# A hand-planned order for a delta-rule layer and a SwiGLU layer: the groups of tiny products ahead of K's turn removed, and the order searched anew

## The chip, the cores and the metric

The kernel runs on one core of a Trainium2 chip. The metric is the time of one execution on the device in microseconds (us); the runs of the kernel before have a median of 670.19 us over three executions (669.39 to 670.93). The core has five engines with a queue each: TensorE (PE, matrix products), VectorE (DVE), ScalarE (ACT), GpSimd (POOL) and SyncE (SP, which here issues most of the transfers). Every engine works through its own queue strictly in the order in which the program wrote it, and waits at the head of that queue for whatever the next instruction needs.

## The reference

```python
def _attn_ref(q, k, v, beta):                 # 4 batches, 8 heads, 768 steps, 48 channels
    k_n = k / (np.linalg.norm(k, axis=-1, keepdims=True) + 1e-06)
    state = np.zeros((B, H, D, D)); y = np.zeros_like(q)
    for t in range(S):
        kt, vt, bt = k_n[:, :, t], v[:, :, t], beta[:, :, t, None]
        y[:, :, t] = einsum('bhd,bhde->bhe', q[:, :, t], state)
        v_old = einsum('bhde,bhd->bhe', state, kt)
        state = state + bt[..., None] * einsum('bhd,bhe->bhde', kt, vt - v_old)

def _moe_ref(x, w_gate, w_val, w_out, rms_g): # x: y as 3072 tokens x 384; 384 -> 1536 -> 384
    xn = x / sqrt(mean(x * x) + 1e-06) * rms_g
    g = xn @ w_gate
    return (g * sigmoid(g) * (xn @ w_val)) @ w_out
```

All data are float32 in the result; the three weight matrices come as float64 and are converted on the chip.

## The kernel before, in words

The 768 steps are cut into 12 chunks of 64 (`NCH`), and each chunk is solved for all 32 heads at once. For a chunk the program normalises k (`norms`), turns k and q so that their channels lie on the partitions (`turn`, a product with the identity, whose line is L560), forms the scores of k against k and of q against k, inverts a triangular 64 by 64 matrix per head, and from that computes the chunk's y and the new state (`recur`). The two first chunks invert with `invert`, the later ones by a longer way in `prep`. Then the SwiGLU layer runs on the chunk's 256 tokens: `ffn_plain` (products L1443 and L1425) in chunks 0 and 1, and in chunks 2 to 11 `ffn` (products L1538) and `down` (products L1595), which need fewer products for more additions on VectorE; the sums that feed L1595 are L1587. The weights are loaded in 18 pieces into seven raw buffers and converted to float32 by two operations on ScalarE (L500, L501), a shift on VectorE (L495) and an addition on POOL (L498) each (`weights`).

Nothing of this is issued where it is written. Every step is an operation of a class `Plan`: an engine, a planned duration, a function that issues it, and the keys that it reads and writes. At the end `Plan.run` takes all operations in the order that a string `ORDER` spells out, two characters for the number of an operation in the order of creation (base 90). There is one string for all engines; each engine's queue is what remains of it for that engine. Before it issues them, `Plan.times` works out planned start times from the planned durations, from a model of the transfers' landings and from a model of how TensorE's instructions are fetched. These times have one effect on the program: which PSUM bank an operation gets, and where *filler* is put. Where the plan leaves PE idle for over 0.8 us in the first 110 us (`UNTIL`), it issues useless wide products with the identity into a free bank (L1714; 4, 2 or 1 times 128 columns), so that they fill the planned gap. Ahead of PE's first operation, where the time since the previous one is counted from 0.0, `fillers` returns a fixed list.

The function `ahead` adds an operation of twelve useless products of one column (L642); `prep` calls it six times in chunk 0. Each counts as 48 of the units in which the plan counts PE's instructions. The order string puts five of the six groups at the very start of PE's queue, ahead of the two halves of K's turn of chunk 0 (L560 on k), and the sixth between the two halves of q's turn.

Around these, the first chunk goes: the transfers of k (one half issued by SP, one by ACT); ScalarE squares k (L604) and VectorE sums the squares (L605); K's turn, copied out of PSUM by ScalarE (L572) and VectorE (L570); scores (L700); a power on POOL for the norm (L609); the transposition and the inversion on VectorE (L734 to L814; L810 is `back`, the transposition back); two rounds of products (L841, L874) and additions (L881); V times beta over the norm (L1155); the products L1212, L1236 and L1190; the mean square and the scale of y (L1308, L1348); y's turn (L1371) and its scaling (L1380); and then the first product of the SwiGLU layer (L1443).

Of the kernel before, what the change touches and what calls it, by code (L numbers as in the profile page):

```python
# [16 lines left out]
C = 64  # L17
W = 32
# [18 lines left out]
    "&-&I%m%,&L'+&(&N%/%'%+%l%j&S%1%k%B&M%-(+&,'$%p'%'G%>&O%q'V''%(%o%r&X%0%n%G'H%2&P#8(*%s#7$~%?#6%@%C'J%u%#&T%w'K%9%t&U"
    "'&&Q%5&R%A%x%4'I&Y%L%z&V%v%y(1%E%D&^#:%:%F&.#;&Z'(%{&['L%|%}%;','M&W%<'N&_'-'P'Q(,%6&`'O&]%M%7'R'/%N&d#9(-#5&a#<'.&6"
    "(.&c)#'0%H%O(/)$&h'S)%&/%J&e&b)&&i%P&f%I&j'T(0&g'1)d&k'A'2&0%K'3&n'C'4'B'W*G&l&7)e'U)g'5'D&o'X'6&s&p'Y'E'Z)f&1'8'[&t"
    "'F)h']'7&q'='^'9&m'_':'>&u'?'`'@)i';'<'a)A&:)k&v)j&8&r'b)l'c)n(?)o'd)m(;(2'e&;(@'f&9'g&w'h(<'i'j&x)''k)q)0)p(=&y(A'l"  # L40
    "(>)C(B(C)1'o(3'm(D'p)2'n(I)B(E)3(7(J)r(F(4(K)(&}&z(N&~(6'w(L'|)=(O'y)s'z)t'}(5(G(S'~(P'{)u(H'x*F)v)w(T't)x'u)y's(#'q"
    "(Q(U)z(M'r($'v){*M(%)|*N(R(()}()'#(&(9(')D)~&|)G(V)E*#(W)I)H)F*$*H(X*%(:(^&2*&(Y*I*J*')J(Z*(*K*)(_**([*+)b,v(c)K(`(8"
    "*,(a(d*L*-)L(h,/)c*/)M*.(e(i*0(f)4,u,2)>(j,0)N(m,1)O)5,3*5))+i*7(k*<*O,4*9*;)?(]*=,5*>,6*:)*(n,A,:)+,B,9),(r,7)6(o,8"
    ")P+k)Q*8(s(p*1)-*3)7*?*2).)V*6)8)R*4)W(b)X,;)9*@(t,<)/)S)T*A*U)Y):)U(g)Z*C);*D*B)[*E+j(l)](u)^+l)<)_)`+o)a+m,=*P,>*V"
    ",?*W,@,w,C*R*S,D(q*Q&{,E,F&3,G,x,H(v,I+p,y,J(w,K*T,z,L*Y,M*[*Z,N*X(x*],O+q*^(|,{*d(}(y(~*_._*`({*e(z*f*a.`*l,P*b.a+&"
    "*g*m,Q*j*n,R*k.b+(,S*o,}*h*p,T,|*v*q+**c,U.c*z++*w*r*i*{+)+2,V*|+n*~*}*x,W+'.d+.,X*s+,,Y,~*t+r,Z+-+3+4+#,]+/+$.e+:*y"
    ",[+%+8+5,^+;*u,_+<+s+9+t/L+@+=+v+>.f+6+u+D+A+w.g+?,c+B)@,j-#,k.i,m+y+H+E,l.h,h+0+L.t+I.j.l,-+x+M,i+F+z.m+7+~+G+{.k+T"
    "+N+C,#,./K,$+J+1.u,b+O+P,g,n,%+|,`+Q+}.;,a+K,o-$.o,p,e,&.=,d+V+R,q,f,',t,(.n+U,),s+S&4,r,*+Z,+.<,,+].>-%+W+^.A.?-*.p"
    ".B.q-,.r/M.s.v+X.C.w+[.x.@.y.z/N.{&5+a.|-(+Y/O.}-&.~/P.D/#+b/$-+--+_/%.^1~+d/Q-..E15+`-0.F-/.].G+e-116/&-)17/'-2+f.H"
    "+c-T+h-3.I+g-6/(18.K-8-7-4.J-</).L->/S/*-=-V-9-?19/+-B-:2#-@-5-C.M-X/,-L-;-Y/--A-D1:-M-W-'-H/.-N/R-O-]-I-U.N-a//-J-E"  # L50
    "/0-P1;-b-Z/1-Q-i-R-[-^/3-c-K/5-S-g1<.O0n/2-h-d/4-j-m-_-e-F1=-n/C-G-k/B/T1?.P1>-o-f-l-`1B-w-p1C-s1@-x1A.'.#-y/X-q-t/A"
    "-z/@-u-r1J.$/>-{/?-v.(/D1E-|/U1D.Q-}/8.)/9-~.R.%/6.S.&/E/<./.T/=1K.U/:.-.V.W/;.X.Y.Z.[.+...0/7/Z0p1F/W1G/F1H/V.31I1L"
    "0o/I/H1M.*/G1N/J1O1P.,1Q0t.41R.11S1T2$1U0v/]1V0q.2/^2%.72&1W0r0u2'1X/_.81Y.9/a/`.51Z0w2)/b0s.61[.:/c2*2(0x/[3h/i0y/d"
    "0z/e/j0{3i/k1]0|4T/q1^0~0+/f/l0-/g0}1_3k/m/o1`1#/s3j/p1a/Y/r0/1b/t/h/u1c3l00/{/v1d/w1$/|0#/n/}1e130.1g070$0'2+3m0%1%"
    "030&1f140,2,081h0(012-0)3D/x3n021q/y0?/~21/z041&090@0*1v0=1u0:4U0E3E0;1j3o0>0A1l051'0<0C060B1i1s3p0D1t0F1r0I3r3q0M0J"
    "3}3u1w0N3t0Q0U3s0O0G3v0Y0P1x0R0K1k1o0L0S0H1m1(1y1n1p0[0V1)3w1z0T1{0W3x1}0b1*1+0`1|0X0Z1,3~1-1.1/100^110a3F0c123J3y3G"
    "3K3z3{0]0f3|4V4#4$0_4%3H4&4'4(0d4W4)0g4X4*0h4+4[234Y4,2/25244-0i27260e4.29284/2;4Z0j2:206>2<2.2?0k406?2A0m2@0l2E2B2^"
    "412F2C2G423I6A2K6@2H43222`2L2I442M452J6B3L2U2D4]2N2b2V2Q462W2a2X3M2=472_6C482O2>492R2d3N2S2Y4:3O2c3Q2e2j3P2Z6D2l2T3R"
    "4>2[2k2f4<2m3T2r3S2g2n3U2t2P2s3g4=6E2p4;2u2h2]2|4^2q4L6F2i3V2o2v3f4K6H6G2x2w6K4_2y6I2}6J3$2z6L2{4E3(3%3W307+3&3)2~6S"
    "3#3'6N3*4a5w313,3X3+326M3.3-4@4I384H365y4J333/3Y344G37394A6T4C5x6O4F6P4M4D6Q3<4B6R3Z6U4N4?356V7,6W4`3[6X6Y3]4b3^6Z4O"  # L60
    "3=723:6[4S3_4d4Q6]4R3`4P3a3b5}3;3c6^5z6_3@7-3d3e5~6#6`5{4e4f7.3A3C4h7/6a4g3B5|4j736b4i703?544k6c3>4l6d4n6e4r716$4m8q"
    "4s4o4t6%8r6&4z8s6f6'4c4x6(4u4{566g6)4y4|6h8t4~6i9_4}4p586j6+6*5#5(4v6,6k5,4w6l5)8u5$4q576<6m59506=5-8M5%5.6q5/5@6-51"
    "558v5&5A525:6o5*746n5<6p5;755=535B8w5+6.5F9^5C5H5'7#5G775J8N6s5I6~5>5L8x5K6z9*6/5N6v5M9+5R6y6{8y6|5S6}5O5V5T608z768{"
# [193 lines left out]
def kernel(  # L257
# [37 lines left out]
    ident = sbt("ident", [128, 128])  # L295
# [171 lines left out]
    def weights(first, last):  # L467
# [14 lines left out]
        for n, (dst, src, keys) in list(enumerate(todo))[first:last]:  # L482
# [19 lines left out]
            P.add("DVE", 0.7, shifted, pr, w=cak)  # L502
# [134 lines left out]

    def ahead(n, pr):

        def small():  # L640
            for _ in range(n):
                nc.tensor.matmul(banks[0][0:32, 0:1], ident[:, 0:32], ident[:, 0:1])  # L642

        P.add("PE", 0.04 * n, small, pr, r=["ident"], size=4 * n)
# [39 lines left out]
    def invert(c, pr):  # L684
# [127 lines left out]
        P.add("DVE", 1.02, back, later(8), r=["two16"], w=["acc16", "xc16"], port=False)  # L812
# [72 lines left out]
    def prep(c):  # L885
# [826 lines left out]
    def filler(n, warm):  # L1712
        for w_ in n:
            nc.tensor.matmul(  # L1714
                warm[:, 0 : 128 * w_].rearrange("p (w n) -> p w n", n=128), ident, ident[:, None, :].to_broadcast([128, w_, 128])
            )
# [33 lines left out]
```

## Time and profile before

| | us |
|---|---|
| median of the runs (lowest to highest) | 670.19 (669.39 to 670.93) |
| the profiled execution's own time | 667.71 |
| its span, first to last instruction | 666.0 |
| PE busy | 658.1 |
| VectorE busy | 537.5 |
| ScalarE busy | 299.5 |
| POOL busy | 168.9 |
| filler products L1714, busy | 28.9 |
| tiny products L642, busy | 5.1 |
| products L1538 / L1595 with all operands, share of the chain that ended last | 40% / 20% |

All durations come from one profiled execution, whose times are counted from its first instruction. In a line of the profile a tile name stands for all buffers of that name, and two counts say what a product's record is: a float32 product is recorded as two matmuls and two weight loads (PEld), a turn as one of each. A wait in square brackets is the idle time of the engine ahead of the instruction, with what ended it.

### The profile page before, as it was taken

What the parts mean: (1) busy time and instruction counts of PE and PEld (TensorE: products, weight loads), DVE (VectorE), ACT (ScalarE), POOL (GpSimd) and SP (SyncE); (2) the same over time, 40 slices, a digit from 0 to 9 for tenths busy, and PEclk for the clock granted to TensorE, in tenths of its full rate; (3) what the DMA queues carried; (4) which work ended last, traced back from release to release, by engine and by line L of the source; (5) the groups of instructions that cost most, each with busy time, mean ns of one, the idle gap of its engine ahead of it and who ended that gap; (6) DMA issues with size and microseconds to landing.
All of it is one profiled execution on the core that took longest, in us unless ns stands there. A gap on an engine that the chain in (4) does not pass through costs nothing.

```text
span 666.0 us, 23581 instructions
## 1 busy us (share of the span) xinstructions
PE 658.1 (99%) x10108; PEld 604.3 (91%) x10108; DVE 537.5 (81%) x1125; ACT 299.5 (45%) x712; POOL 168.9 (25%) x219
## 2 busy tenths in 40 slices
PE   9999999999999999999999999999999999999997
PEld 6678788778799999899999999999999999999997
DVE  2978779989898798988898898899898898458463
ACT  2777844235346344354445345445344344253240
POOL 0564783121510510520510340420410300000000
PEclk8999999999999999999999999999999999999999
DMA  9587764556565586186355666467545434120101
GB/s 210 172 197 258 200 157 91 91 115 93 103 118 85 143 160 113 22 159 106 76 93 109 100 127 109 88 130 108 84 98 84 73 75 71 30 58 9 26 1 24
DMA packets 270584, 69.38 MB, mean 104 GB/s; under 512 B 257488, under 2 KB 262736, under 8 KB 270160
## 3 DMA queue, kind: packets, MB, share of 16 engines
q1 hardware_dynamic: 269360, 67.63, 50.7%
q8 instruction: 79, 1.29, 0.9%
q10 hardware_dynamic: 1120, 0.25, 0.2%
q14 instruction: 25, 0.20, 0.1%
HBM read 49.76 MB, written 22.02 MB: 108 GB/s over the span
## 4 chain that ended last, share of the span: by engine, by line
PE 93%; DVE 4%; ACT 2%; issue 1%; POOL 0%; POOLq 0%; DVEq 0%; ACTq 0%
PE bank L1538 40%; PE bank L1595 20%; PE bank L1443 8%; PE bank L1425 4%; PE bank L1714 4%; PE bank L1113 3%; PE bank L583 3%; PE bank L1190 2%; PE bank L1176 2%; PE bank L1283 1%; PE bank L560 1%; PE bank L1055 1%; PE bank L1075 1%; PE bank L642 1%; PE bank L841 1%
## 5 line engine op out<-in xcount | busy, mean ns | idle before, releaser
L1538 PE MATMUL bank<-xf,w_in 128*128 128x128 f32 x1440 | 180.3, 276 | 0.0
L1538 PEld LDWEIGHTS bank<-xf,w_in 128*128 128x128 f32 x1440 | 170.0, 192 | 1.7 <-issue 0.2
L1548 DVE TENSOR_TENSOR tmp<-tmp,bank 128x512 f32<-128x512 f32 x180 | 120.8, 683 | 46.1 <-PE bank L1538 30.3
L1538 PE MATMUL bank<-xf,more 128*128 128x128 f32 x960 | 123.1, 276 | 0.0
L1550 ACT COPY tmp<-bank 128x512 f32<-128x512 f32 x120 | 68.3, 586 | 107.2 <-PE bank L1538 82.1
L1538 PEld LDWEIGHTS bank<-xf,more 128*128 128x128 f32 x960 | 114.8, 192 | 0.8
L1554 ACT ACTIVATE tmp<-tmp 128x256 f32<-128x256 f32 x120 | 47.2, 414 | 65.5 <-DVE tmp L1548 65.0
L1006 DVE TENSOR_REDUCE acc<-acc 128x30 f32<-128x90 f32 (+4 forms) x150 | 71.0, 473 | 5.2
L1595 PE MATMUL bank<-wo_sb,hf 128*128 128x192 f32 x360 | 64.0, 330 | 0.0
L945 POOL TENSOR_TENSOR at<-at,beta_b 128x256 f32<-128x256 f32 (+3 forms) x32 | 20.2, 661 | 162.9 <-DMA at<-dkk 112.4
L1595 PEld LDWEIGHTS bank<-wo_sb,hf 128*128 128x128 f32 x360 | 58.1, 190 | 1.2 <-issue 0.4
L1000 DVE TENSOR_TENSOR acc<-acc,at 128x60 f32<-128x60 f32 (+4 forms) x150 | 52.8, 352 | 6.1 <-DMA dq<-in_q_dram 2.8
L1555 DVE TENSOR_TENSOR hf<-tmp 128x256 f32<-128x256 f32 x120 | 47.0, 416 | 2.8 <-ACT tmp L1554 2.2
L628 POOL TENSOR_TENSOR knrm<-ksum,half 128x16 f32<-128x16 f32 x11 | 32.2, 2931 | 44.0 <-DVE ksum L607 43.7
L1026 POOL COPY acc<-acc 128x128 f32<-128x128 f32 x40 | 17.4, 464 | 81.2 <-DVE acc L1006 80.6
L1425 PE MATMUL bank<-wo_sb,hf 128*128 128x384 f32 x96 | 34.4, 493 | 0.0
L1443 PE MATMUL bank<-xp,w_in 128*128 128x256 f32 x144 | 33.7, 384 | 0.4 <-ACT xp L1380 0.4
L1395 DVE TENSOR_TENSOR xf<-xf 128x256 f32<-128x256 f32 (+1 forms) x70 | 30.2, 462 | 4.3 <-ACT xf L1365 3.0
L1443 PE MATMUL bank<-xf,w_in 128*128 128x256 f32 x144 | 32.8, 380 | 0.0
L1443 PEld LDWEIGHTS bank<-xf,w_in 128*128 128x128 f32 x144 | 27.1, 190 | 5.0
L1443 PEld LDWEIGHTS bank<-xp,w_in 128*128 128x128 f32 x144 | 26.5, 190 | 4.5 <-issue 0.6
L1714 PE MATMUL bank<-ident 128*128 128x512 f32 (+2 forms) x82 | 28.9, 499 | 1.4 <-POOL ident masks.py:199 1.4
(221 smaller groups left out, 1009.0 us busy)
## 6 DMA issues: line engine op xcount, KB each, us to landing
at<-dkk SPq DMA_DIRECT2D x20, 256.0 KB, 3.9
vt<-in_v_dram SPq DMA_DIRECT2D x24, 192.0 KB, 4.0
k<-in_k_dram SPq DMA_DIRECT2D x23, 192.0 KB, 3.7
out_dram<-tmp SPq DMA_DIRECT2D x46, 96.0 KB, 2.2
dks<-k SPq DMA_DIRECT2D x14, 256.0 KB, 2.8
kt<-dks SPq DMA_DIRECT2D x28, 128.0 KB, 3.5
more<-in_moe_w_gate_dram SPq DMA_DIRECT2D x4, 768.0 KB, 8.2
more<-in_moe_w_out_dram SPq DMA_DIRECT2D x4, 768.0 KB
```

The lines of the kernel that those rows point to most:

```text
L628: P.add("POOL", 2.95, lambda: nc.gpsimd.tensor_tensor(out=knrm[i2], in0=ksum[i2], in1=half, op=ALU.pow), pn, r=[("ksum", i2), "half"], w=[ ...
L1000: nc.vector.tensor_tensor(out=acc[:, 1:3, 0:n, j + 2 : W].rearrange("p a i t -> p i a t"), in0=acc[:, old, 0:n, j : j + 2, None].to_broadc ...
L1006: nc.vector.tensor_reduce(out=acc[:, new, 0:n, j + 2 : W], in_=acc[:, lo : lo + 3, 0:n, j + 2 : W].rearrange("p a i t -> p i t a"), axis=A ...
L1425: nc.tensor.matmul(po[p].t[:, 0:DM], hf[:, spot(f), 128 * p : 128 * p + 128], wo_sb[:, spot(f)], start=(f == f0), stop=(f == f1 - 1), skip ...
L1443: nc.tensor.matmul(ps.t[:, TOK * side : TOK * side + TOK], w_in[:, side, h_, 3 * t + i_, n : n + 128], x_[:, 2 * t : 2 * t + 2].rearrange( ...
L1538: nc.tensor.matmul(g.t[:, 128 * z : 128 * z + 128], fac[:, side, 128 * f : 128 * f + 128], xf[:, xs], start=(begin and z == 0), stop=False ...
L1548: P.add("DVE", V(512), lambda t=t, g=g: nc.vector.tensor_tensor(out=t, in0=t, in1=g.t, op=ALU.add), -1, r=[g], w=[tk], last=g)
L1550: P.add("ACT", A(512), lambda t=t, g=g: nc.scalar.copy(t, g.t), -1, r=[g], w=[tk], last=g)
L1554: P.add("ACT", A(256), lambda t=t: nc.scalar.activation(out=t[:, 0:256], in_=t[:, 0:256], func=ACTF.Silu), -1, w=[tk])
L1555: P.add("DVE", V(256), lambda t=t, f0=f0, p=p: nc.vector.tensor_tensor(out=hf[:, spot(f0) : spot(f0) + 2, 128 * p : 128 * p + 128], in0=t[ ...
L1595: nc.tensor.matmul(g.t[:, 0:192], a_[:, f], b_[:, f], start=(begin and f == 0), stop=(f == 5), skip_group_check=True)
L1714: nc.tensor.matmul(warm[:, 0 : 128 * w_].rearrange("p (w n) -> p w n", n=128), ident, ident[:, None, :].to_broadcast([128, w_, 128]))
```

## The change

Four things change.

1. `ahead` and its six calls are gone: 72 tiny products.
2. `fillers` returns, ahead of PE's first operation, two wide products and thirteen tiny ones instead of two wide ones and one of half the width; `filler` issues a tiny product for an entry 0.
3. Two planned durations are others: the shift L495 is planned with 0.62 instead of 0.70, the transposition back L810 with 1.20 instead of 1.02.
4. The string `ORDER` is another one: it comes from a search that uses the planned durations alone, without errors in the landings of transfers.

With the numbers behind the six groups moved by six, the two strings can be compared. The longest part that keeps its order leaves out, of each engine's operations: PE 132 of 568, ACT 236 of 627, DVE 317 of 920, POOL 15 of 162, SP 253 of 499. No operation moves by more than 11 places on PE, 18 on ACT, 45 on DVE, 11 on POOL and 45 on SP. In the new order PE's first operations are the two halves of K's turn, then the scores L700.

```diff
 ORDER = (
-    "#.#'#-#S#)#h###R#,#e#(#4#d#*#/#g#f#3#0#1#a#W#H#_#b#`#X#C#r$#$?#Y#&#Z$@#u#s#>#T#v#t#U#V#$#{#i#c#k#[#|$q#j#}#z#^#l#~#y"
...
+    "#.#'#-#&#R#+#)###S#$#y#,#3#(#/#*#4#0#C#a#W#H#_#b#`#X#l#Y$9#Z#M$:#m#o#T#n#p#U#V#u#c#2#e$;#[#v$<#>#w#r#^#f#x#t#z$k#{#d"
...
 )
 def fillers(a, b):
     if a == 0.0:
-        return [4, 4, 2]
+        return [4, 4] + [0] * 13
...
-            P.add("DVE", 0.7, shifted, pr, w=cak)
+            P.add("DVE", 0.62, shifted, pr, w=cak)
...
-    def ahead(n, pr):
-
-        def small():
-            for _ in range(n):
-                nc.tensor.matmul(banks[0][0:32, 0:1], ident[:, 0:32], ident[:, 0:1])
-
-        P.add("PE", 0.04 * n, small, pr, r=["ident"], size=4 * n)
-
...
-        P.add("DVE", 1.02, back, later(8), r=["two16"], w=["acc16", "xc16"], port=False)
+        P.add("DVE", 1.2, back, later(8), r=["two16"], w=["acc16", "xc16"], port=False)
...
         if c == 0:
-            for n in range(6):
-                ahead(12, 14.0)
             P.urgent = 300.0
...
     def filler(n, warm):
         for w_ in n:
+            if not w_:
+                nc.tensor.matmul(warm[0:32, 0:1], ident[:, 0:32], ident[:, 0:1])
+                continue
             nc.tensor.matmul(
                 warm[:, 0 : 128 * w_].rearrange("p (w n) -> p w n", n=128), ident, ident[:, None, :].to_broadcast([128, w_, 128])
             )
```

More of the change, by code (lines that the diff above doesn't have):

```diff
@@ L37 @@
[L37 to L51, printed above, removed]
@@ new lines @@
+    "#}#|#g#q#]#~#D#8#I$##1#s$$$f#J$%$($)$=$'$&$*%K#N$,$+$.$-#@#K$/#F#?#L%N$3$p$2#=#k#A#O$>#E#P$l$?#i#G$4$A$@%O#h#Q%L&#$5"
+    "$6$g#j$B%M$a#B$h%x$C$D$E%y$F$G$q$u$i$H$I$J%P$K$n$S$L$s$T&$$M$U$N$0$V$m#%%T$O$z$7$j$W$X$P%Q$R$Y$Q$Z$[$]$1$o&6%R$c%#&7"
+    "$b%S%U$d%z$^%V#:&8%W$e&:%(%{%X$8&B&;%Z&9%Y%|&>%[&<%]%}%_&?%^$w%`$_&%$`$r&=%a'#&@%-$|&D%b(%'$${#<&&$t&C%$&'%7%c&H&0%%"
+    "$}%g&E%d%f%e%~'%&A&z$v%&%h%'&F%j%2&}%<&{&M%k&(&G$~%*%i&I%l%)($$x&J'P%+$y#5%m%A&K&N%3%o'A%n%/%p%q&O%8&~%,'B&P'D&R'E%:"
+    "%9%r&L%.%;&S%t%s%F'C%=#6&|%u#;%>&)%?&W%4%w%@&Q&T&1%0'F%v%1&U'&'G'H'?&X%5'(')'K%6''(&'I&]'L'*'J'@&Y%G&*('#7%H((';%I%B"
@@ new lines @@
+    "&V(y'+()%C%D'M&Z(z#9&^*A({(|&b',%E'-&_&['=%J'N&c&`&+'Q(+&d'.(*&,&a'/)^&g&e&f'<'0&h'O'>'2)a'1'R)_'7&m'S'8&4'T&2'U&n'V"
+    "'W'3&o&i'X'9)b'Y'4'5&l)`':'Z&j'6)c'[&5);&k)e'])d(5&p)f'^)h&q&3'_)g&r'`)i(,(6'a*@'b&s(7'c'd(9&t'e)k(8)*)j(:&w)+'f(=(;"
+    "(<(-(>'i'g)=(C'j),(?)-'h(D(@&y(}&x(~)>(3(E)<)7'k(.'u's(A)l(H't)m'w(0(I'x)n(F'v(/'l(M(4)o(J*G(N(K)p'o)q'm)r'y'n)s(B(1"
+    "'z)t(O'p'r)u'{'q(G*H)v'~'}'|)w(#(L(2(P)x)A)y(W)C)?)z*B(R)B)@){(S*C(X*D(T)|(U)D*E(Y)})~(]*#*$,p(Q*%&v*F)E(^*&(Z)F)[(b"
+    ")G,))]*)(_*I)H*'(c**)I)#*(,*(`)8,,)K,o(g(d,-).,++c)/)J*,)0*3,.)9*6*-(h*8,/(e*.)1,0*7(l)2(i*2+d,4)$(m,3)%,1)&,2)P)L)3"
@@ new lines @@
+    "*4)Q*9)R*+)')M,;(V*5(j*1)()S(n*/)4)N([)O*:,5)),<*0(o(a,6)T)5)U+e*;)V*J)W*>)X*?)Y,w*=+f*<*L&-+i*K&u)6(f)Z,7,q,8*Q,9,:"
+    ",=*S*R,>,?,r+g(k,@,A*T,B+j*U,C,s,D(p*V,E,t,F(q,G(r,H,I*W(v,u*^(x(s*O*X.X*Y(u*_(t*`*Z(w*|,J.Y*[.Z*d*a,v,K*f*M*e*b*~,L"
+    "*g.[*j,M+$*k*h*c*],N*t+%+k,O*l*i.]+#*u*p*N+h,P*v*P+(*w,Q*}+,,R+&*m.^,S*q+l*n+',T+-*x*o,W+)+.+m._+**y*r+4,U+/*z,X+2*s"
+    "+n,V+5*{+6+p,x/F+3+:+7+++8.`+o,c+0+>+q,e+9,b.a+;,^+s+?+r,f,y):,[.c,d.b+B,g.n,'.g+F+C+<.d+@.e+t+=+x,(,`+u+N+G.f+A,a+H"
+    "+1+v/E+J+D+y,h+w+K,_+z+{.5,Z+I,i+L,]+E,Y+|,j+O,{.h+P+M.i,l+},n,z,k,m.6.o.7+T+~+Q+V/M,#.;,$+U/L,%,&.8+W&.,~.j-$/G.k-&"
@@ new lines @@
+    ".l.m.p+R.q/H.r.s.t.<.u+Z.v+S/I.9.w-'.x/J+X+[.y-%&/.=+].z.:-#-(.{.>.|/K+Y-*1/.?-).@+_.W-+10.}11-0+`+^.~.B,|-,.A-1+b-2"
+    "+a.C--12-8/#-..D-6.E-3.F/$-N-7-4-/-:-9/%-<13-5/&-P-=.G-R-Q/'-;-F.V-S->14-G-V/(.H-H/),}-B-I-Z-O-C/*-T15-[-D/+-J-?.I-U"
+    "-c-E/,-W-]-d//-K-@-a/.-L16/-0h1y-M-A17-b-^.J0j-g-_18-X-e19-h-i/N-f/=1D-q/:-`-j1<-m-r1:-}1;-s-n-k1=-Y/<-o-l-t/2-p-u/9"
+    "-y/8.#0i/1-v/;.K1>-w1?/>-x.L-{/3/O-z/7/?.M.)/4.N/@1E/6.O.'/R.P.Q/C/P/A/5-~/B/0-|.R.S.%.T.(/D.*1x/Q1@.-.$1A1B.&1C1F1G"
+    "0n1H..1I1J.01K0k/T0o1L.U.+1M1z1N1O/V1{/U/X1|1P/W0l/Z.,/Y1}1Q0p.10m1R1S/].2/[1T.40q2$1~1U/_/^3b/c0r0s/e/`0t3c/d0%0u./"
@@ new lines @@
+    "/f/S0v/i1V.30'1W0x0w/k1X3e/j/m0y/g1Y/a3d/o1Z/n/l1[0)/b1]/p/u3f/h1./y1^0(2#/v0*/q0z/z/}1b/{/|012%0&3g0-/w1_020+1a/r1`"
+    "2&/s0,/x091-3h0.030{/~0:2)070#040/1k0?0$1h2(081p0;/t3w4N3i0=1c0<0|053>1o061l0@3j1g2'0A1m0>0C1n3k3@1f3l0G0}0D3o1q0E0H"
+    "3p0K001r3n0F3x3m0B0S3?0I4O0J1e0L1i1s0~1j0M0U1d0N1t3r0Q1v1#0O3q1$1w0[2+1%0Y0T1u1&0P0V0R3D1'1(1)1*3A0]0W1+3B1,3F3s0Z3C"
+    "3t2,4P3u2-3v3y4U0X3z0`3{3|4Q3}3~4#2/0a4R4$0c0^4%200b2.4S4&4'210_254(22234)294T3E0d68242:26692;4*0e0f2?2<0g2A6:4+2@27"
+    "2C4,2=6;2E4-2B2*2W2D2F2G4.2O282H6<2Y2P2I3G4/2Q2>2R402X2[3H6=3I2^2]417%2Z2K2_4V3K2d423J2L432f3L2J2e2`6>442g3N2M2S3M2a"
@@ L81 @@
+    "@B?u@E@D?v@I?w@F@h@J@O@K@P@Q@L@U@R@M@j@G@V@S@N@`@T@k@l@a@p@H@b@m@c@[@i@t@]@n@u@d@o@W@q@e@v@X@f@|@Y@w@z@g@x@Z@^@y@~@_"
+    "@{A$A#@}A*A%A&A+A.A,A'A2A-A(A/@rA:A)A0A1A3@sA<A4A;A5A6A7A?A8A=A9ALADAKA>ABAAAFACAEA@AMAGAHAJAIANAPAO"
 )
```

52 lines of the change are left out of this document (20 added, 32 removed).

## The prediction

> **What bounds the kernel now.** I read the page's head first, then the waits of TensorE, then its busy time over the long stretch after the first FFN product.
>
> ```profile
> span 666.0 us, 23581 instructions
> PE bank L1714 <- POOL ident masks.py:199: 1.4, 1, 1.4
> PE bank L1595 <- DVE xp L1587: 0.9, 1, 0.9
> PE bank L1371 <- ACT yn L1353: 0.6, 1, 0.6
> PE bank L841 <- ACT mt L821: 0.4, 1, 0.4
> PE bank L1443 <- ACT xp L1380: 0.4, 1, 0.4
> PE bank L1212 <- DVE mt L881: 0.3, 1, 0.3
> 50.10:666.00 615.90, 610.12 (x9266) 570.38 (x9266) 506.53 (x1042) 271.15 (x643) 147.93 (x198) 1.00 0.49 97
> ```
>
> The columns of the last row are the stretch, its length, then busy time (and count) of PE, PEld, DVE, ACT and POOL, the granted clock, the DMA share and GB/s. From 50.10 us on PE is busy for 610.12 of 615.90 us; in that stretch the waits are 0.9 + 0.6 + 0.4 + 0.4 = 2.3 us, the rest being the stores behind the last product. So the time is when that stretch begins plus work that the change leaves alone. The busy share of 99% hides the other half: part of what PE does before 50.10 us is filler. The timeline of PE shows it (start, duration, then what ran and how many records; a float32 product is two records):
>
> ```profile
> 1.42 4.63 PE L1714 MATMUL bank<-ident 128*128 128x512 f32 x6 [1.42 <-POOL ident masks.py:199]
> 5.98 4.23 PE L642 MATMUL bank<-ident 128*32 128x1 f32 x120
> 10.14 3.38 PE L1714 MATMUL bank<-ident 128*128 128x512 f32 x8
> 13.35 1.04 PE L560 MATMUL bank<-ident,k 128*128 128x128 f32 x8
> 14.23 1.25 PE L1714 MATMUL bank<-ident 128*128 128x512 f32 x4
> 15.40 1.16 PE L700 MATMUL bank<-kt 64*64 64x64 f32 x64
> 18.38 0.92 PE L642 MATMUL bank<-ident 128*32 128x1 f32 x24
> 19.72 2.54 PE L1714 MATMUL bank<-ident 128*128 128x512 f32 x8
> ...
> 46.59 1.57 PE L1714 MATMUL bank<-ident 128*128 128x512 f32 x6
> 48.00 0.85 PE L1371 MATMUL bank<-ident,yn 128*128 128x128 f32 x6
> 48.68 1.04 PE L560 MATMUL bank<-ident,q 128*128 128x128 f32 x8
> 50.10 5.42 PE L1443 MATMUL bank<-xp,w_in 128*128 128x256 f32 x24 [0.38 <-ACT xp L1380]
> ```
>
> K's turn is L560 on k, at 13.35 us. ScalarE and VectorE say when its data were there and who waited for it:
>
> ```profile
> 5.86 0.84 ACT L604 ACTIVATE r<-k 128x768 f32<-128x768 f32 x1 [2.82 <-DMA k<-in_k_dram]
> 14.43 0.59 ACT L572 COPY kt<-bank 128x512 f32<-128x512 f32 x1 [7.73 <-PE bank L560]
> ...
> 13.99 0.69 DVE L570 COPY kt<-bank 128x512 f32<-128x512 f32 x1 [11.66 <-PE bank L560]
> 14.60 0.94 DVE L605 TENSOR_REDUCE ksum<-r 128x16 f32<-128x768 f32 x1
> ```
>
> K had landed by 5.86 us, when ScalarE squares it. PE could have turned it then; instead it worked through sixty tiny products (120 records) and a filler queued in front. VectorE sat idle for 11.66 us and ScalarE for 7.73 us, and even the sum of squares L605, which needs no turn, stood in VectorE's queue behind the copy L570. The whole solution of chunk 0 hangs on that chain, so the stretch at 50.10 us starts about 7.5 us later than K's landing asks for. This is the stage in which the change is priced.
>
> **The change part by part.**
>
> *What stands ahead of K's turn.* Decoded, the new order has K's turn as PE's first operation; the six groups are gone. `fillers` is then called with a = 0.0 for K's turn itself and returns two wide products and thirteen tiny ones, nothing more, so nothing else can stand there. The first filler of before is lengths 4, 4, 2, ten units in 5.98 - 1.42 = 4.56 us, 0.456 a unit; eight units take 3.65 and end at 5.07. A tiny record takes (10.14 - 5.98)/120 = 0.035 us; 26 records take 0.90 and end at 5.97, or at twice that price 1.80, at 6.87. Earlier than 5.9 K is not there. So K's turn moves from 13.35 to between 5.9 and 6.9; I take 6.4: **-6.95** (-7.45 to -6.45).
>
> *The sixth group.* 0.92 us at 18.38, between the two halves of q's turn. PE runs 2.54 us of filler right behind (19.72), so its removal is worth 0; without that filler it would be worth 0.9 more.
>
> *From K's turn to the first FFN product.* Before it takes 50.10 - 13.35 = 36.75 us. PE, ScalarE and VectorE keep nearly the same order here (of PE's 568 other operations 132 change their place, none by more than 11), so I let it shift whole, and bound three terms.
>
> ```profile
> 45.85 0.76 ACT L1348 ACTIVATE yn<-bank,rs 128x192 f32<-128x192 f32 x2
> 33.93 2.61 DVE L1155 TENSOR_TENSOR vt<-vt,rb 128x768 f32<-128x768 f32 x1
> 33.89 1.83 POOL L498 TENSOR_TENSOR w_in<-more 128x768 uint32<-128x768 uint32 x1 [0.66 <-DVE rb L619]
> 7.37 0.67 SPq L402 DMA_DIRECT2D vt<-in_v_dram  x1
> 14.96 5.20 SPq L402 DMA_DIRECT2D wsum<-in_moe_w_gate_dram  x1
> ```
>
> First, yn was ready at 45.85 + 0.76 = 46.61, but its turn L1371 began at 48.00 behind a filler: 1.39 us lost. In the new order a half of q's turn stands in that gap, and less filler can: -1.4 to 0. Second, VectorE's product L1155 lasted 2.61 us beside a POOL addition of 1.83 us. The Trainium skill, "SBUF — State Buffer", on the shared port pair, says that a VectorE operation with two SBUF inputs and a GpSimd operation lock each other out for a whole instruction; this trace has the product once, beside POOL, so it shows the length and not the rule; by that page alone the sum would change by one POOL addition either way. The new order puts L1155 behind three weight shifts L495 and two L881, with the two first additions of POOL ahead and a third behind it: it can save about one addition or wait for one more, -1.8 to +1.8. Third, one half of V (issued at 7.37) moves on SP's queue behind five weight loads and a load of beta, about where the issue of the gate weights took 5.20 us. L1155 needs V at 33.93 - 6.95 = 26.98. Issued at 14.96 + 5.20 = 20.16 at the latest, it has 6.8 us to land: 0. Of the three together I take **0**, with -3 to +3.
>
> *Queues passed.* On SP 253 of 499 loads and stores change places, on POOL 15 of 162 operations. Of the loads that the chain of chunk 0 needs only V comes much later.
>
> *Planned durations.* 0.62 for 0.70 (L495) and 1.20 for 1.02 (L810) issue no instruction. They set the order and the later fillers only; 0 of their own.
>
> *The rest of the order.* From 50.10 us on, the same operations in another order, chosen without errors in landings. The change leaves the kinds of work on PE alone, and counted in the decoded lists, PE changes between large and small products 209 times instead of 205: nothing. What can come is waits. The 2.3 us of before may all go, -2.3; on the other side one wait as the longest seen, 0.9, in each of nine later chunks is +8.1. Chunks 2 to 11 had 0.9 + 0.6 = 1.5 in before; an order with no reserve should show somewhat more, and I take **+1.0**, near the rows of before.
>
> The sum is -6.95 + 0 + 1.0 = -5.95. The profiled execution took 667.71 us (span 666.0, 1.7 around it), so 661.8 for a like execution. The runs shown have a median of 670.19, 2.5 above it; the same step from there gives **664.2 us**.
>
> **The rivals.**
>
> *The weights set the pace.* The first six weight loads start with the kernel, not with K's turn. If they, and the eighteen conversions after them, don't move with the chain, chunk 0's products wait for their weights and the gain is swallowed.
>
> ```profile
> GB/s 0 11 218 170 160 146 138 186 200 272 387 400 390 393 382 403 356 215 242 279 97 36 0 0 13 0 0 0 180 376 216 122 68 157 160 172 141 277 371 403
> 36.34 0.93 ACT L500 ACTIVATE more<-wsum 128x768 f32<-128x768 f32 x1
> SPq L402 <- ACT tmp L501: 25.7, 4, 13.8
> ```
>
> The first row covers 0 to 50 us in slices of 1.25. The first batch has landed by 27.5 us (the 22nd slice); its last buffer is taken up for conversion in before at 36.34, in the new order at about 29.4, still behind its landing. And SP waits 25.7 us for conversions (third row), so later loads start when buffers come free, which shifts with the chain. Against it, therefore; if it held in full, 6.95 of gain would go and the 1.0 of waits stay: 671.2; in part, about 669. Chance 0.13.
>
> *Slower: a wait once per chunk.* The place is L1595 behind L1587, where the second-level sums of `down` are made on VectorE while PE has only a few products in between. The new order spreads these products among those of L1538 (25 passages from L1538 to L1595 instead of 15) and has been searched as if each transfer landed on time. At 0.9 us each, the gain of 6.95 is gone from the eighth wait on; in each of ten chunks, with as much again at a second place in half of them, it is 13.5 us: 670.19 - 6.95 + 13.5 = 676.7. For it speaks that before shows just this wait once and that VectorE is busy 506.53 of 615.90 us; against it, that nine chunks of before went without it. Chance 0.12.
>
> *A cold clock at K's turn.*
>
> ```profile
> 6.13:9.54 3.41, 3.41 (x111) 3.41 (x111) 0.00 (x0) 0.57 (x1) 0.00 (x0) 1.00 1.13 155
> 9.55:12.95 3.40, 3.40 (x19) 2.17 (x18) 0.00 (x0) 0.00 (x0) 0.00 (x0) 0.50 1.07 245
> 12.96:20.00 7.04, 7.04 (x122) 5.90 (x121) 5.61 (x15) 3.54 (x10) 2.91 (x1) 1.00 1.06 393
> ```
>
> The granted clock was 1.00 while the tiny products ran, 0.50 in the 3.4 us behind them, and 1.00 again after a stretch of wide ones: tiny products do not hold the clock. In the new order wide ones stop at 5.07, and the turn and the scores may run at 0.50. At most they double: 1.04 (13.35) + 1.16 (15.40) = +2.2, so 666.4. The Trainium skill, "TensorE: Matmul & The Clock Gate", section on the clock gate, says that the window of 3.4 us runs free of the kernel's start, so by it both cases would occur from one execution to the next; the rows show steps of 3.41 us, and one execution cannot show their phase. Chance 0.13.
>
> **How the numbers follow.** The forecast, the gain of K's turn coming through with about a microsecond of new waits, has 0.62; its own range is 661.0 (no waits and the filler at L1371 saved) to 667.5. The three rivals have 0.13, 0.12 and 0.13. 0.2% is 1.3 us, about what a measurement of this kernel can tell from no change. Faster by more than that (under 668.9): the forecast, the cold clock, and the milder part (0.05) of the weights, 0.80. Within: 0.07, the rest of the weights but its upper edge (0.01). Slower: 0.12 and that edge, 0.13. The range 661.0 to 670.0 leaves out some 0.06 below and 0.13 above.
>
> **What would show it.** In the profile after: four wide filler records, 26 tiny ones, and K's turn at about 6.4 us; L570's idle time at 4 to 5 instead of 11.66; L605 right behind it; the first L1443 at about 43.2 (42 to 46); and from there a stretch of 615 to 618 us. Step one is wrong if K's turn comes after 7.5. The weights rival shows as waits of L1443 for POOL's L498; the slower rival as waits of L1595 or L1538 for VectorE chunk after chunk, with the stretch longer than 623 us; the cold clock as 0.50 in the stretch that holds L560 and L700. The prediction as a whole is wrong if the first L1443 comes early and the end does not.

## The result, and the profile after

| | before | after |
|---|---|---|
| median of the runs, us (lowest to highest) | 669.79 (669.22 to 670.93), 4 runs | 662.86 (662.63 to 663.93), 4 runs |
| the profiled execution's own time, its span | 667.71, 666.0 | 663.93, 662.2 |
| K's turn starts (L560 on k) | 13.35 | 6.60 |
| first FFN product starts | 50.10 | 44.21 |
| from there to the end | 615.9 | 618.0 |

The ratio is 0.9898, with a 95% interval of 0.988 to 0.9915: 6.9 us less, faster by more than the 0.2% that can be told apart. The prediction was 664.2 us. Lines behind the removed function have numbers lower by 8, from the removed calls on by 10, and the filler's by 7 (L1714 is now L1707): L700 is L692, L841 L833, L1212 L1202, L1443 L1433, L1595 L1585, L1155 L1145.

The timeline of TensorE of the changed kernel, with the lines that answer to those of before (start, duration, what ran, number of records, idle time ahead):

```profile
1.41 3.78 PE L1707 MATMUL bank<-ident 128*128 128x512 f32 x4 [1.41 <-POOL ident masks.py:199]
5.12 1.55 PE L1705 MATMUL bank<-ident 128*32 128x1 f32 x26
6.60 1.97 PE L560 MATMUL bank<-ident,k 128*128 128x128 f32 x8
8.36 1.96 PE L1707 MATMUL bank<-ident 128*128 128x512 f32 x4
10.25 1.16 PE L692 MATMUL bank<-kt 64*64 64x64 f32 x64
...
17.62 1.16 PE L583 MATMUL bank<-qt,kt 64*64 64x64 f32 x64 [0.65 <-ACT qt L572]
...
32.50 1.15 PE L1202 MATMUL bank<-vt,mt 64*64 64x48 f32 x64 [0.79 <-DVE vt L1145]
...
36.96 1.14 PE L1707 MATMUL bank<-ident 128*128 128x256 f32 x6
39.13 1.14 PE L1707 MATMUL bank<-ident 128*128 128x256 f32 x6
43.35 1.03 PE L1707 MATMUL bank<-ident 128*128 128x256 f32 x4
44.21 2.75 PE L1433 MATMUL bank<-xp,w_in 128*128 128x256 f32 x12
```

Four wide records, 26 tiny ones, then K's turn: 6.75 us earlier. The chain behind it is shifted nearly whole, 37.61 us instead of 36.75. New in it are two waits (0.65 and 0.79), and the turn itself lasted 1.97 us instead of 1.04. ScalarE and VectorE show the other side of the same move:

```profile
5.79 0.84 ACT L604 ACTIVATE r<-k 128x768 f32<-128x768 f32 x1 [2.50 <-DMA k<-in_k_dram]
8.60 0.58 ACT L572 COPY kt<-bank 128x512 f32<-128x512 f32 x1 [1.98 <-PE bank L560]
7.75 0.69 DVE L570 COPY kt<-bank 128x512 f32<-128x512 f32 x1 [4.69 <-PE bank L560]
8.36 0.94 DVE L605 TENSOR_REDUCE ksum<-r 128x16 f32<-128x768 f32 x1
```

L570's idle time fell from 11.66 to 4.69 us and L572's from 7.73 to 1.98, and the sum of squares L605 runs right behind. The page's head, TensorE's waits (total, times, longest), and two stretches (length, then PE, PEld, DVE, ACT, POOL busy with counts, granted clock, DMA share, GB/s):

```profile
span 662.2 us, 23310 instructions
PE bank L1585 <- DVE xp L1577: 1.7, 1, 1.7
PE bank L1103 <- ACT state L1399: 1.0, 1, 1.0
PE bank L1433 <- DVE hf L1442: 0.9, 1, 0.9
PE bank L1415 <- issue: 0.6, 1, 0.6
PE bank L1585 <- issue: 0.4, 1, 0.4
44.21:662.20 617.99, 609.67 (x9267) 569.36 (x9266) 507.26 (x1042) 271.73 (x643) 152.15 (x200) 1.00 0.50 97
57.58:60.99 3.41, 3.41 (x8) 2.16 (x7) 3.38 (x6) 2.90 (x5) 1.49 (x2) 0.50 0.83 237
```

Behind the first FFN product these five waits make 4.6 us where before had 2.3. They alone aren't why the stretch grew by 2.1 us: the same kernel profiled again (e8 and e11 below) has 3.8 and 4.2 us of such waits and a stretch of 615.5 and 616.4 us. What this profile has besides is the slow clock of the last row. The clock fell to 0.50 for one window of 3.41 us behind L1103's wait, and the products there (L1433, then L1415) took 2.35 and 3.70 us, against 1.56 and 2.74 in e8: 1.75 us more. In e8 and e11 the same wait of 1.0 us was there and the clock stayed at 1.00. What the longer waits cost is made up elsewhere: TensorE is busy for 608.0 (e8) and 608.3 us (e11) in this stretch, where before had 610.12. Why it is less stays open.

### The profile page after: what moved, and what is told of

Its sections match the earlier page's. It is cut to its first block, busy times and chain, and to the rows that moved or that the text cites. A ratio compares the mean times of both kernels' runs of the same rounds, so it can differ in the third digit from the quotient of the medians.

```text
span 662.2 us, 23310 instructions
## 1 busy us (share of the span) xinstructions
PE 650.7 (98%) x9976; PEld 597.9 (90%) x9976; DVE 538.9 (81%) x1125; ACT 300.1 (45%) x712; POOL 172.1 (26%) x219
## 4 chain that ended last, share of the span: by engine, by line
PE 92%; DVE 4%; ACT 2%; issue 1%; POOL 0%; DVEq 0%; POOLq 0%; ACTq 0%
PE bank L1528 41%; PE bank L1585 20%; PE bank L1433 8%; PE bank L1415 5%; PE bank L1103 3%; PE bank L583 3%; PE bank L1707 2%; PE bank L1180 2%; PE bank L1166 2%; PE bank L1273 1%; PE bank L560 1%; PE bank L1045 1%; PE bank L1065 1%; PE bank L833 1%; PE bank L866 0%
## 5 line engine op out<-in xcount | busy, mean ns | idle before, releaser
L1585 PE MATMUL bank<-wo_sb,hf 128*128 128x192 f32 x360 | 64.0, 329 | 0.0
L935 POOL TENSOR_TENSOR at<-at,beta_b 128x256 f32<-128x256 f32 (+3 forms) x32 | 22.0, 718 | 158.1 <-DMA at<-dkk 139.1
L1585 PEld LDWEIGHTS bank<-wo_sb,hf 128*128 128x128 f32 x360 | 58.1, 190 | 1.2 <-issue 0.4
L1415 PE MATMUL bank<-wo_sb,hf 128*128 128x384 f32 x96 | 35.6, 504 | 0.6 <-issue 0.6
L1433 PE MATMUL bank<-xp,w_in 128*128 128x256 f32 x144 | 35.2, 390 | 0.9 <-DVE hf L1442 0.9
L1433 PE MATMUL bank<-xf,w_in 128*128 128x256 f32 x144 | 33.1, 383 | 0.0
L1433 PEld LDWEIGHTS bank<-xp,w_in 128*128 128x128 f32 x144 | 27.0, 192 | 6.3 <-DVE hf L1442 1.3
L1433 PEld LDWEIGHTS bank<-xf,w_in 128*128 128x128 f32 x144 | 26.9, 190 | 4.3
L1322 POOL TENSOR_SCALAR ms<-ms 128x2 f32<-128x2 f32 x11 | 3.6, 331 | 93.6 <-ACT bank L1310 93.6
```

What stands on the lines that cost most here:

```text
L1415: nc.tensor.matmul(po[p].t[:, 0:DM], hf[:, spot(f), 128 * p : 128 * p + 128], wo_sb[:, spot(f)], start=(f == f0), stop=(f == f1 - 1), skip ...
L1433: nc.tensor.matmul(ps.t[:, TOK * side : TOK * side + TOK], w_in[:, side, h_, 3 * t + i_, n : n + 128], x_[:, 2 * t : 2 * t + 2].rearrange( ...
L1585: nc.tensor.matmul(g.t[:, 0:192], a_[:, f], b_[:, f], start=(begin and f == 0), stop=(f == 5), skip_group_check=True)
```

## The experiments

The theory: the gain is K's turn, nearly 7 us earlier, because of the work taken from in front of it. The first rival: the new order brings the gain. The second: the thirteen tiny products matter by themselves, as a delay or by what they do to the clock or to TensorE's supply of instructions. Every kernel ran beside the kernel before, which had medians of 668.88, 671.01, 669.68 and 668.87 us on the four chips (e1 to e4, e5 to e8, e9 and e10, e11 and e12). So ratios are compared, not times.

| kernel | median | ratio (95%) | K's turn | first FFN product | waits for "issue" ahead of it | filler behind L1202 |
|---|---|---|---|---|---|---|
| before | 669.79 | 1 | 13.35 | 50.10 | 0 | 4.3 |
| after | 662.86 | 0.9898 (0.988 to 0.9915) | 6.60 | 44.21 | 0 | 3.3 |
| e1 | 665.87 | 0.9958 (0.9933 to 0.9984) | 6.61 | 47.71 | 0.5 | 7.1 |
| e2 | 679.1 | 1.0117 (1.0072 to 1.0161) | 13.61 | 56.84 | 1.9 | 8.5 |
| e3 | 663.66 | 0.9895 (0.9853 to 0.9938) | 7.55 | 45.37 | 2.5 | 3.3 |
| e4 | 667.7 | 0.9953 (0.9927 to 0.9979) | 5.83 | 50.14 | 1.8 | 8.5 |
| e5 | 666.78 | 0.9941 (0.9908 to 0.9974) | 13.44 | 49.37 | 0 | 3.3 |
| e6 | 663.36 | 0.988 (0.9814 to 0.9946) | 5.84 | 45.37 | 1.5 | 4.3 |
| e7 | 663.61 | 0.988 (0.9823 to 0.9937) | 5.77 | 45.85 | 2.8 | 3.3 |
| e8 (after again) | 662.87 | 0.9869 (0.9813 to 0.9925) | 6.24 | 46.09 | 4.4 | 3.3 |
| e9 | 662.09 | 0.9886 (0.9853 to 0.9919) | 6.28 | 42.73 | 1.3 | 0 |
| e10 | 660.69 | 0.9857 (0.9831 to 0.9883) | 5.84 | 43.28 | 1.6 | 0 |
| e11 (after again) | 662.37 | 0.9889 (0.9856 to 0.9922) | 6.60 | 44.26 | 0 | 3.3 |
| e12 (e10 again) | 660.77 | 0.9871 (0.9833 to 0.991) | 5.84 | 42.77 | 1.1 | 0 |

The four columns on the right come from each kernel's timeline of TensorE; the last two are summed from it, up to the first FFN product (in the numbering of before, filler is counted behind L1212).

**e1: order of before, new head.** The changed kernel with the string of before (numbers moved by six) and the two planned durations of before.

```diff
 ORDER = (
-    (the new string)
+    (the string of before, without the six groups)
 )
...
-            P.add("DVE", 0.62, shifted, pr, w=cak)
+            P.add("DVE", 0.7, shifted, pr, w=cak)
...
-        P.add("DVE", 1.2, back, later(8), r=["two16"], w=["acc16", "xc16"], port=False)
+        P.add("DVE", 1.02, back, later(8), r=["two16"], w=["acc16", "xc16"], port=False)
```

> The order string, the planned durations and everything else of before; only the six groups are gone and the head is that of the change (two wide products, thirteen tiny ones, then K's turn). Theory (the gain is K's turn coming early): K's turn at 6.6 us, the first FFN product some 6 to 7 us ahead of 50.1, and 663 to 664 us, as with the change. Rival (the gain comes from the new order): 669 to 670 us. If the new order itself costs the 2 us by which the stretch after the first FFN product grew (615.9 to 618.0), this kernel is faster than the change, 661 us.

**e2: new order, a head as long as before.**

```diff
-        return [4, 4] + [0] * 13
+        return [4, 4, 2] + [0] * 60 + [4, 2, 1, 1]
```

> The changed kernel with before's head: ten units of wide filler, sixty tiny products and eight more units of filler ahead of K's turn, in the new order. Theory: K's turn at about 13.4 us and 669 to 671 us. Rival (the new order gains by itself): 663 to 665 us although K's turn is late.

**e3: half the delay.**

```diff
-        return [4, 4] + [0] * 13
+        return [4, 4] + [0] * 13 + [4, 4]
```

> The changed kernel with two more wide products (eight units) between the thirteen tiny ones and K's turn. Theory: K's turn 3.4 us later if the clock is low there (0.43 us a unit), 1.7 if it is high, and the time later by the same amount: 664.6 to 666.3 us. If the chain behind K's turn had slack (waits on landings of V, q or the weights), the time would grow by less than the turn: under 664.

**e4: no tiny products.**

```diff
-        return [4, 4] + [0] * 13
+        return [4, 4]
```

> The changed kernel without the thirteen tiny products. If they are mere delay, K's turn comes with K's landing at 5.8 us instead of 6.6 and the time falls by 0.8, to 662.1 us. If they serve the fetch of TensorE's instructions (52 instructions ahead of everything), some waits that the profile puts down to issue get longer and the time rises by 0.5 to 2 us.

These four didn't settle it; e1, e2 and e4 landed in none of the ranges that were expected. e1 had K's turn at 6.61 us and was only 0.4% faster than before, where the change is 1.0% faster. e2 lost more than its delay: its turn comes 0.26 us behind that of before, its first FFN product 6.7 us. e4, with K's turn earliest of the four, lost half of the gain. The timelines say why: each of them changes the number of instructions ahead, and the plan answers. Of e1 and then e4, TensorE:

```profile
34.52 0.31 PE L833 MATMUL bank<-mt,m1bd 64*64 64x32 f32 x5 [0.46 <-issue]
34.76 4.14 PE L1707 MATMUL bank<-ident 128*128 128x512 f32 x12
47.71 4.55 PE L1433 MATMUL bank<-xp,w_in 128*128 128x256 f32 x20 [0.38 <-ACT xp L1370]
```

```profile
35.63 1.26 PE L1226 MATMUL bank<-u,kk 64*32 64x48 f32 x50 [0.46 <-issue]
36.82 3.29 PE L1707 MATMUL bank<-ident 128*128 128x512 f32 x10
42.65 1.15 PE L692 MATMUL bank<-kt 64*64 64x64 f32 x60 [1.34 <-issue]
43.72 4.14 PE L1707 MATMUL bank<-ident 128*128 128x512 f32 x12
50.14 2.11 PE L1433 MATMUL bank<-xp,w_in 128*128 128x256 f32 x9
```

The planner's `times` models when TensorE's instructions arrive, in blocks counted in units of the plan (`fetch`). Where it foresees an operation held up by a block, it takes what hangs on that operation for late and has wide filler issued in the gap: 4.14 us of it in e1 at 34.76 (before has none there), 3.29 and 4.14 us in e4. The wait that came was 0.46 us, or 0.46 and 1.34. So the filler for a foreseen wait seems to have cost more than the wait (e7 tests this for e4). Edits of the head are confounded with the plan unless plan and count are held. e3 keeps the filler of the changed kernel, has its turn 0.95 us later, and matches it (ratio 0.9895), which is the case of slack that was named for it: waits behind the turn, 2.5 us of them for "issue", hide so small a delay.

**e5: the new order, the same number of instructions ahead, a late turn.** Fifteen wide products (nine of 512 columns, six of 128) instead of two wide and thirteen tiny; everything behind them is issued as in the changed kernel.

```diff
-        return [4, 4] + [0] * 13
+        return [4] * 9 + [1] * 6
```

> The changed kernel with wide products in the place of the tiny ones: fifteen entries as before, so that every instruction of TensorE behind K's turn keeps its place in the fetched blocks and the plan puts the same fillers everywhere else; only K's turn comes later, at 12 to 13 us instead of 6.6. Theory A (the gain is K's turn): the first FFN product moves from 44.2 to 50 or 51 us and the time is 669 to 670 us. Theory B (K's turn has slack; what counts is where the blocks of instructions begin, and the filler that the plan adds for them): the time stays at 662 to 664 us.

**e6: the order and plan of before, an early turn.** Five of the six groups and the filler ahead of the two halves of K's turn are planned and not issued.

```diff
-                if op.fill:
+                if op.fill and op.n not in (59, 61):
...
-        P.add("PE", 0.04 * n, small, pr, r=["ident"], size=4 * n)
+        P.add("PE", 0.48, small, pr, r=["ident"], size=48)
...
-                ahead(12, 14.0)
+                ahead(0 if n else 12, 14.0)
```

> The kernel before with its order, its planned times and all its other fillers, but the five groups ahead of K's turn and the filler behind them are planned and not issued (256 instructions of TensorE fewer ahead of K's turn, near one fetched block of 16 KB). Theory A: K's turn at 6.0 instead of 13.35, the first FFN product at 43 to 44 us and 662 to 663 us, the whole gain of the change without its order. Theory B, that the groups hold off a wait for instructions: waits put down to issue appear in the first 45 us, 4 us or more in sum, and the time is 666 us or more.

These two settle the main question in part. First TensorE and the stretch of e5, then of e6:

```profile
13.44 1.04 PE L560 MATMUL bank<-ident,k 128*128 128x128 f32 x8
49.37 2.75 PE L1433 MATMUL bank<-xp,w_in 128*128 128x256 f32 x12
49.37:665.00 615.63, 608.23 (x9267) 568.88 (x9265) 505.53 (x1042) 271.64 (x643) 150.30 (x200) 1.00 0.50 97
```

```profile
5.84 1.24 PE L560 MATMUL bank<-ident,k 128*128 128x128 f32 x8
11.14 0.63 PE L560 MATMUL bank<-ident,q 128*128 128x128 f32 x4 [0.60 <-DMA q<-in_q_dram]
33.87 0.36 PE L841 MATMUL bank<-mt,m1bd 64*64 64x32 f32 x9 [0.90 <-issue]
38.79 0.55 PE L1190 MATMUL bank<-u,pt 64*64 64x48 f32 x20 [0.58 <-issue]
45.37 5.42 PE L1443 MATMUL bank<-xp,w_in 128*128 128x256 f32 x24 [0.36 <-ACT xp L1380]
45.37:661.50 616.13, 610.35 (x9266) 570.34 (x9266) 506.45 (x1042) 270.80 (x643) 147.19 (x197) 1.00 0.50 95
```

The old order with an early turn has the whole gain (0.988, beside 0.9869 for the changed kernel on the same chip). So the move of K's turn is enough for it. The first FFN product came later than the 43 to 44 us expected, behind 0.6 us of waiting for q and 1.5 us for "issue". The new order with a late turn takes 3.9 us more than the changed kernel (666.78 against 662.87 in e8); its time lies between the two ranges that were expected. Behind the first FFN product the two orders take 616.1 and 615.6 us: in these profiles the order is worth nothing there.

e5 is still faster than before, by 0.3 to 0.9%, which is 4.2 of the 8.1 us between the medians on this chip (671.01, 666.78, 662.87). By the profiled executions it is only 1.0 us (665.0 against 666.0), 0.7 of it ahead of the first FFN product. The rest is in the longer executions of before, of which there is no profile. So the early turn is enough for the gain, but by the medians it isn't shown that the whole gain is lost without it, and what else makes before's executions long stays open.

**e7: tiny products planned, not issued.**

```diff
             if not w_:
-                nc.tensor.matmul(warm[0:32, 0:1], ident[:, 0:32], ident[:, 0:1])
                 continue
```

> The changed kernel in which the thirteen tiny products are planned and not issued: the plan and all other fillers are those of the change, but 52 instructions fewer reach TensorE. It parts two readings of the 5.6 us that their removal cost. If the cost is the filler that the plan adds for a wait it foresees, K's turn comes at 5.8, the first FFN product at 43.5 to 44.5 and the time is 661.5 to 663.5 us. If it is a real wait for instructions, waits put down to issue of 2 to 4 us stand behind L1226 and L692 and the time is 664 to 667 us.

**e8: the changed kernel again**, unedited, beside e5 to e7.

> The changed kernel itself, for a comparison on the same chip: 0.99 of the kernel before under either theory, 661 to 664 us.

Without the tiny products but with their plan, the ratio is 0.988: e4's loss was its filler (8.5 us behind L1202 against 3.3), not the missing products. The other reading was half right: e7 lost its lead at K's turn (5.77) to one wait of 2.83 us for "issue" at L692, but its time stayed that of the changed kernel beside it. And e8, the very kernel of the first profile, shows what that profile by chance did not, TensorE:

```profile
6.24 1.09 PE L560 MATMUL bank<-ident,k 128*128 128x128 f32 x8
11.03 1.07 PE L560 MATMUL bank<-ident,q 128*128 128x128 f32 x8 [1.11 <-DMA q<-in_q_dram]
34.35 0.32 PE L833 MATMUL bank<-mt,m1bd 64*64 64x32 f32 x7 [2.13 <-issue]
40.92 0.49 PE L1180 MATMUL bank<-u,pt 64*64 64x48 f32 x18 [2.24 <-issue]
46.09 2.75 PE L1433 MATMUL bank<-xp,w_in 128*128 128x256 f32 x12
46.09:661.60 615.51, 607.99 (x9267) 568.68 (x9266) 506.27 (x1042) 271.63 (x643) 150.86 (x200) 1.00 0.49 95
```

Its turn was earlier and at full clock, and its first FFN product later by 1.88 us: 4.37 us went to two waits inside runs of like products (57 of 64, then 7). The instruction queue says what they were. In e8 two packets of that queue end at 32.90 and 39.39 us; the waits end at 34.35 and 40.92, 1.45 and 1.53 us behind. The 14 profiled executions hold 29 waits of TensorE for "issue" of 0.25 us and more; every one ends 1.2 to 1.8 us behind the end of a packet of the instruction queue, though these packets come some 8 us apart. By this they are waits for blocks of instructions, though no run moved a block alone. In e5, whose instructions stand at the same places in the blocks and whose turn comes 7.2 us later than in e8, the third packet ends at 37.66 us instead of 32.90. So when the chain runs 7.2 us earlier, this block comes only 4.8 us earlier.

**e9 and e10: the last wide filler not issued**, in the changed kernel (e9) and in e6 (e10): the groups that the plan puts behind its 33 us. In e10 the condition stands beside that of e6.

```diff
-                if op.fill:
+                if op.fill and s < 33.0:
```

> The changed kernel with its last three groups of wide filler products not issued: the ones ahead of L1180, of the second L692 and of the first FFN product (1.14, 1.14 and 1.03 us, 16 records, in the profile of after at 36.96, 39.13 and 43.35 us). Everything else, the plan too, is as it was. Theory A (they stand in waits that the plan foresees from its own durations, but behind the wait for instructions the chain is late for other reasons, and so they are in the way): the first FFN product comes up to 3.3 us earlier, at 41 to 44 us, and the kernel takes 659.5 to 662. Rival B (they fill true waits for VectorE and ScalarE): waits of 0.5 to 1.1 us appear ahead of the same three places, the first FFN product stays at 44 to 46 us, 662 to 664. Rival C (the waits for TensorE's instructions grow by what is left out, because the instructions ahead run sooner than the blocks arrive): waits put down to issue of 3 us and more, 662 to 665.

> The order of before with the early turn (the kernel e6_old_plan_early_turn: five groups of tiny products and the filler behind them planned and not issued), and in addition without the groups of wide filler ahead of L1190, of the second L700, of L1371 and later ones of the head (1.14, 1.57 and 1.57 us there). Theory A (they are in the way): first FFN product 1.5 to 4 us ahead of its 45.37 us, 659.5 to 662. Rival B (true waits): 45 to 46 us, 663 to 664. Rival C (waits for instructions grow instead): issue waits of 3 us and more, 663 to 665.

**e11 and e12: the changed kernel and e10 side by side**, unedited.

> The changed kernel itself, unedited, on the same chip as the next run, so that the two can be compared. Its three earlier medians or single comparisons were 0.990 and 0.987 of before. Theory A (the gain is K's turn, the rest is waits that vary): ratio 0.986 to 0.991, first FFN product between 44 and 46 us, waits for TensorE's instructions between 0 and 4.5 us from one execution to the next. Rival (the order after the first FFN product is worth something by itself): the stretch behind the first FFN product shorter than 615 us.

> The kernel e10 again (order of before, five groups of tiny products and the filler behind them not issued, the last groups of wide filler of the head not issued), beside the changed kernel on one chip. Theory A (early turn in the old order, and the late filler was in the way): 1.5 to 2.5 us less than the changed kernel beside it, ratio to before 0.984 to 0.988, first FFN product at 42.5 to 44 us. Rival (e10's lead was the chip's or chance): within 1 us of the changed kernel beside it.

TensorE of e12:

```profile
5.84 1.76 PE L560 MATMUL bank<-ident,k 128*128 128x128 f32 x8
33.63 0.36 PE L841 MATMUL bank<-mt,m1bd 64*64 64x32 f32 x9 [0.75 <-issue]
36.44 1.53 PE L1190 MATMUL bank<-u,pt 64*64 64x48 f32 x50 [0.38 <-DVE u L1250]
40.56 0.97 PE L1371 MATMUL bank<-ident,yn 128*128 128x128 f32 x6 [0.90 <-ACT yn L1348]
42.77 4.55 PE L1443 MATMUL bank<-xp,w_in 128*128 128x256 f32 x20 [0.36 <-ACT xp L1380]
```

In the old order 4.28 us of filler (e6) gave way to waits of 0.38 and 0.90 us: the first FFN product came 2.1 (e10) and 2.6 us (e12) earlier, of which up to 0.6 is e6's second wait for "issue", gone in e10 and 0.30 in e12. That the filler was in the way is shown by both profiles. What it is worth in time is less sure. e10 and e12 have 660.69 and 660.77 us, against 662.37 for the changed kernel beside e12; the means of these two, six runs each, differ by 1.3 us (95% interval from 3.1 less to 0.4 more). So the version faster than both is likely, not proven, against the changed kernel; against before it is proven. In the new order (e9) the first FFN product came earlier too, at 42.73, with waits of 0.37 and 0.55 us where filler had been, but its ratio of 0.9886 can't be told from the changed kernel's 0.9869 to 0.9898.

## Why the prediction was right, step by step

**K's turn.** Right: 6.60 us, taken as 6.4, bounds 5.9 to 6.9. The 26 tiny records took 1.55 us, between the two prices of 0.90 and 1.80. That this move is enough for the gain is shown by e6 (the move alone). e5 (all but the move) loses about half of the gain by the medians, and most of it by the profiles, so the two don't add up to one account of the medians.

**The sixth group at 0.** In agreement: e6 kept it and matched the changed kernel. It wasn't tried alone.

**From K's turn to the first FFN product, 0 (-3 to +3).** +0.86 in the profile after, +3.1 in e8, +2.8 in e6: in part at the upper edge of the bounds or just past it, and mostly not by the terms that were named. This is the step that was wrong in kind. The prediction let the stretch shift whole and looked for delays in three places. Two others came. The blocks of instructions are next late: the chain runs 7 us earlier, the blocks follow only in part (4.8 of 7.2 us from e5 to e8), and waits of up to 4.4 us appear. And q's landing, up to 1.1 us (e8): of the loads that the chain needs, the prediction looked only at V, whose later load caused no wait.

Of the three terms, the second was real. VectorE's product of V and beta runs beside an addition of POOL, in the profile after, then in e8:

```profile
29.88 2.56 DVE L1145 TENSOR_TENSOR vt<-vt,rb 128x768 f32<-128x768 f32 x1
29.68 1.95 POOL L498 TENSOR_TENSOR w_in<-more 128x768 uint32<-128x768 uint32 x1
```

```profile
28.19 0.94 DVE L1145 TENSOR_TENSOR vt<-vt,rb 128x768 f32<-128x768 f32 x1
28.43 2.37 POOL L498 TENSOR_TENSOR w_in<-more 128x768 uint32<-128x768 uint32 x1 [0.58 <-ACT more L501]
```

Where the addition began first the product took 2.56 us, near before's 2.61; where the product began first it took 0.94 us and the addition was the longer one. That is 1.6 us one way or the other within one kernel, and of these two executions only the slow one has the wait of 0.79 us for this product. The filler ahead of yn's turn, where 0 to 1.4 us was to be had, is gone there, but other groups of filler remained; e10 and e12 put the price of such groups at 2.1 to 2.6 us in the old order.

**The order behind, +1.0 (-2.3 to +8.1).** +2.1 in the profile after, -0.4 in e8 (615.5), +0.5 in e11 (660.7 - 44.26 = 616.4). The term varies from one execution to the next as much as it is large, and that the profile after is near it is partly luck. The waits came, 1.5 to 2.3 us more than before where +1.0 was forecast. But 1.75 us of the profile after's +2.1 is its slow window of the clock, and TensorE's busy time there, which the prediction left as it was, is 2 us shorter in e8 and e11; without the slow window the term is about 0.

**The sum.** Profile against profile it was -5.95 predicted and -3.78 measured (667.71 to 663.93): 1.0 us short ahead of the first FFN product, 1.1 behind it. The medians differ by 6.9. The step from the profile to the median, taken as +2.5 for both kernels, failed: before's profiled execution was among its quickest, and after's was the slowest of its four. The profiled execution came 2.2 us later than its forecast of 661.8, and the step from it to the median was -1.1 instead of +2.5. So 664.2 against 662.86 is close partly because two errors cancel, and that is luck. Why before's executions scatter upward (667.65 to 675.71 in all runs here) stays open.

**The rivals.** *The weights set the pace*: no; no product of L1433 waits for a weight, only once for hf (0.9). *A wait once per chunk at L1595*: the wait is there, 1.7 us, once and not per chunk. *A cold clock at K's turn*: by the durations this did occur in the profiled execution. The turn took 1.97 us instead of 1.04 (+0.93) and the wide filler behind it 1.96 instead of 1.25 (+0.71), while the scores took 1.16 as before; so the scores began 3.65 us behind the turn instead of 2.05, which is 1.6 of the +2.2. The sign that was named for it, a granted clock of 0.50, can't be read there: the profile's record of the clock begins only with a rise to 1.00, at 9.79 us in the profile after and at 5.66 us in e8. The slow turn occurred in e11 too (1.97, with the rise at 10.43 us) and not in e8 (1.09) or e9 (1.09). The Trainium skill, "TensorE: Matmul & The Clock Gate", Part 1, has the window run free of the kernel's start, and these executions of the same head agree: the rise comes at 5.66, 9.79 or 10.43 us, with nothing different in the kernel. Against the prediction's price, the two profiles of the changed kernel with the cold turn have the earlier first FFN product (44.21 and 44.26 against 46.09) and no wait for instructions. Whether the slow turn is what lets the blocks arrive in time wasn't tried.

## What to carry to other kernels

When an engine is busy all the time, look at what it is busy with ahead of the first long chain; work that could run and stands behind useless work in the same queue is worth its whole delay, less what is late next (here waits for instructions and for q, which left 4.0 of 7.1 us at the first FFN product in e8). An edit to a planned kernel changes the plan as well: to price one part, hold the plan and leave only the issue out, as e6 and e7 do, since e1 and e4, which let the plan answer, would have given the gain to the wrong cause. And one profile of a kernel whose executions differ by 2 us at its head isn't enough to say what its waits are; take the same kernel twice.

## What the runs showed that was not expected

TensorE can run out of instructions with no branch in the program. The page of the changed kernel counts what its instruction queue moved (packets, MB, share of the DMA engines):

```profile
q8 instruction: 78, 1.28, 0.8%
```

That is 16.4 KB a packet. The Trainium skill, "Runtime: NRT & Kernel Launch", section on instruction fetch mechanics, has blocks of 16 KiB, which this agrees with, and calls their cost mostly hidden because instructions are issued more slowly than they come in. The measurement differs: waits of 2.13 and 2.24 us within one head (e8), 2.83 (e7), each ending 1.45 to 1.53 us behind the end of a packet. Nothing in the list of waits names the queue; the releaser reads "issue".
